# Summing the complex product before the inverse transform, in every second inverse step of an SSM-convolution and gated-MLP block

## The chip, the cores and the metric

The kernel runs on one core of a Trainium2 chip. The metric is device time in microseconds, the median of several executions. The engines that matter here are TensorE (PE in the profile; its weight loads are PEld), VectorE (DVE), ScalarE (ACT), GpSimd (POOL) and the DMA queues that SyncE (SP) issues.

## What is computed

The reference is a block with two branches, cut here to what matters (2048 positions, 640 channels, everything in bfloat16 from outside):

```python
def _A_ref(q, k, v, shift_k, ssm_k, ssm_D):          # long convolution, gated by q
    k_shift = sum over t of k shifted by t * shift_k[:, ks - 1 - t]     # 4 taps   (cut)
    kv = k_shift * v
    kv_f = rfft(kv padded to 2 S)                     # along the sequence, float32
    kf_f = rfft(ssm_k padded to 2 S)
    y = irfft(kv_f * kf_f)[:S]                        # the complex product
    y = y + kv * ssm_D
    return q * y

h = _layernorm(x) * (1 + ca) + sa                     # ca, sa, ga, ... from silu(c) @ w_mod
x = x + ga * _A_ref(h, A_k, A_v, A_shift_k, A_ssm_k, A_ssm_D)
h = _layernorm(x) * (1 + cb) + sb
x = x + gb * _B_ref(h, ...)                           # gelu MLP with a [S, S] spatial mix
```

The change lies in the first branch: in the complex product and the inverse transform that follows it.

## The kernel before

The long convolution is a transform in two stages, written as matmuls. The 640 channels are worked in five units of 128 (`DU`); each unit has eight steps (`NST`) of two frequency blocks (`KP`). For each step, `forward` multiplies the first stage's result by the table `M2` into PSUM, once for the filter (`k_item`) and once for the signal (`u_item`). The filter's result is copied to SBUF as `KH`, in bfloat16. Then VectorE multiplies the signal's real and imaginary parts by the filter's in all four combinations, and TensorE multiplies the four products by the inverse tables `G2` and adds them up in PSUM:

```python
def forward(name, X1, st, extra=()):
    def fn(e):
        pu = new(name, "pu", [P, KP, 2, DU], F32)
        ...
        for k in range(KP):
            kc = st * KP + k
            mm(pu[:, k], M2[:, 0, kc, :], x[:, 2 * kc:2 * kc + 2, :], True, False)
            mm(pu[:, k, 0], M2[:, 2, kc, :], x[:, 2 * kc + 1, :], False, False)
            mm(pu[:, k, 1], M2[:, 1, kc, :], x[:, 2 * kc, :], False, True)
...
def u_item(u, st):
    ...
    def product(e):                                                  # VectorE, line 447
        T_ = new(T, "T", [P, KP, 2, 2, DU])                          # bfloat16
        e.tensor_tensor(T_[:], tl[pu][:, :, :, None, :].to_broadcast([P, KP, 2, 2, DU]),
                        tl[KH][:, :, None, :, :].to_broadcast([P, KP, 2, 2, DU]), op=ALU.mult)
    op("D", "prod", product, r=[pu, KH], w=[T], new=[(T, "T")])

    def inv(e):                                                      # 12 matmuls in a step
        ...
        for k in range(KP):
            kc = st * KP + k
            mm(p_[:, k], G2[:, 0, kc, :], T_[:, k, 0], True, False)          # 256 columns
            mm(p_[:, k], G2[:, 1, kc, :], T_[:, k, 1], False, False)         # 256
            mm(p_[:, k, 1], G2[:, 2, kc, :], T_[:, k, 0, 0], False, False)   # 128
            mm(p_[:, k, 0], G2[:, 1, kc, :], T_[:, k, 0, 1], False, False)   # 128
            mm(p_[:, k, 1], G2[:, 0, kc, :], T_[:, k, 1, 0], False, False)   # 128
            mm(p_[:, k, 0], G2[:, 3, kc, :], T_[:, k, 1, 1], False, True)    # 128
    ...
    op("AD", "zc", ...)      # ScalarE or VectorE copies the result from PSUM into Z
```

Alongside run the four taps and the product with v (`tv`, line 517), a layer norm of x, its modulation `ghm` (line 623: `gh * gca`, then `+ gsa`, on GpSimd or VectorE), a multiplication of `gh` by the inverse transform's result (`ym`, line 640), and a residual add `res` (line 660, GpSimd or VectorE). For the last unit the result Z is transposed on TensorE and kept in tiles `ZT`. Then come the gated MLP's first product (line 237 with `big` and `Z`), its spatial mix (line 918) and its output product (line 936).

All matmuls of the first part go through one helper (`mm`, line 237) and all copies through another (`copy`, line 240), so a line of the profile holds several kinds of work and the tile's name tells them apart.

Nothing is scheduled while it runs: every piece of work is recorded as an operation with the engines that may run it ("GD" is GpSimd or VectorE), and a long list `ORDER` says, operation by operation, on which engine it goes and in which order the engines get their work:

```python
FILLS = (4, 4, 4, 1, 2, 1, 1, 1, 3, 1, 2, 2, )       # matmuls without a use, placed by ORDER
SLOTS = dict(X=4, X1=4, KH=9, T=4, Z=3, ZT=1, wm=1, big=2, dg=2, st1=2, s1=1, sm=2, pu=2, pz=2)
ORDER = """
D13 D95 D12 D96 S14 D97 ...                          # (cut: 991 entries)
"""
```

`SLOTS` gives the number of buffers of each kind.

Of the kernel before, what the change touches and what calls it, by code (L numbers as in the profile page):

```python
# [10 lines left out]
ALU = mybir.AluOpType  # L11
# [4 lines left out]
P = 128  # L16
# [9 lines left out]
DU = 128  # L26
# [7 lines left out]
FILLS = (4, 4, 4, 1, 2, 1, 1, 1, 3, 1, 2, 2, )  # L34
SLOTS = dict(X=4, X1=4, KH=9, T=4, Z=3, ZT=1, wm=1, big=2, dg=2, st1=2, s1=1, sm=2, pu=2, pz=2)
# [4 lines left out]
D13 D95 D12 D96 S14 D97 D103 D109 D104 D110 A0 D115 A5 A4 A1 A2 A3 A111 D98 A99 D6 D18 P979 P980 P981 P19 S16 A112 P21  # L40
D7 D8 D9 S77 D81 S78 A10 D11 G124 G125 D20 P139 A106 D82 D141 P142 A105 A140 A144 P982 P145 A146 D22 G31 D143 D116
D121 A100 G101 A118 S15 P983 P25 S17 D26 P148 S467 P23 D24 S27 A117 G107 A150 P127 D128 A149 A147 S29 G102 P984 P151
A152 P153 A154 S28 G113 S30 G119 P133 A120 G108 P157 A158 P985 P163 S79 A164 P165 A166 D471 D472 P130 D134 P155 A156
G114 P159 A131 D473 D474 P36 G43 D135 P161 D37 A160 P38 D39 P986 P167 D168 A162 A169 G129 P170 A172 P34 A171 S80 P176
A177 D178 P173 D175 P32 A174 S83 P179 D35 P187 P136 D85 P211 D180 D33 G132 P181 S468 D188 D182 A212 P191 P215 P189
A216 D192 S41 A190 P203 D204 P217 A218 P193 A194 D137 P195 S40 D196 P207 S42 P213 D208 D138 P46 P183 D184 P50 A475
P199 S84 A476 D477 D47 A214 P205 A206 P197 D200 A198 P235 A236 P221 D478 A222 D51 P44 P239 A240 P219 A220 D479 G480
P209 A210 P237 S470 D486 P223 P231 A238 A232 D45 P48 A224 D487 P241 A242 D49 S509 P510 A511 P512 A513 D488 D481 A493
S86 D88 D497 P243 D244 A498 G67 D494 P229 A230 P275 G55 A276 P201 D202 P225 A226 P185 S469 S52 D482 P263 P279 A280
P245 A186 A246 D264 D495 S514 P251 D252 P267 S87 P277 A278 D499 D268 P265 A266 P255 A122 D256 P281 A282 D500 P515 P247  # L50
D248 A483 D496 P517 D516 D537 P289 A290 D518 P299 A300 A489 P253 D254 S53 S54 P269 G616 D484 D485 G556 D490 G491 P301
A302 P62 P233 A234 D123 P227 D63 D492 A270 A228 P60 P303 P283 A304 P295 A284 D501 D502 D61 A296 P249 G558 P305 A505
S519 P293 D506 P287 A288 D507 A294 P56 A250 D57 S65 D503 P58 D59 D504 P297 A306 S89 P291 D91 P520 D535 A298 G539 P307
A292 D308 D521 G540 P339 A340 A508 G541 G536 P271 P522 D523 P257 D272 G599 P319 D320 P341 A342 P309 A310 D258 P315
D316 P343 A344 P335 D336 P68 P345 S66 D69 P273 A274 G538 D542 P259 G557 D260 P321 S64 P285 A346 D322 D562 S543 P544
D545 G563 P72 D73 A286 G595 P261 A262 P546 P347 A348 D547 P331 D332 D620 S90 P363 A364 P548 D560 P337 A338 P317 A318
G559 D549 P367 P550 D551 G554 A368 P359 A360 P327 D328 D552 G597 P70 P369 P361 A362 G655 G656 P311 P329 A330 P323 D370
D312 D324 P74 D75 D71 P351 A352 D651 S697 P365 A366 P325 A326 P357 A358 S92 D94 P333 A334 S564 D561 P565 D566 G618
G598 P371 D372 S76 S93 P403 A404 P349 A350 P567 D568 G657 D596 P313 P355 P569 A356 G619 P387 D570 G593 A314 P407 G553
A408 D388 P379 D380 P571 D572 P373 A374 P405 A406 P375 D376 P381 G578 D581 P409 A410 P391 A382 P353 D392 A354 D579  # L60
P389 G573 D576 P427 A428 P395 S601 G653 D654 A390 P377 A378 D396 P429 D600 P399 D400 P397 P383 D384 G594 S698 P602
D603 G583 A430 P431 S524 A432 P423 A424 D587 P401 A402 P415 A416 P433 A434 G588 G617 P604 D577 D575 D398 D605 P425
A426 P411 A412 D652 P393 D574 A394 P435 D436 P419 A420 P606 D607 P385 G658 P451 D452 P443 D444 D582 P608 P437 D438
A386 P417 A418 P525 P421 A422 P447 G614 G615 A526 S622 P453 A454 D609 D613 D448 P455 D456 P445 A446 P463 D464 P449
P459 P457 D460 D580 G611 G621 A450 P413 D610 A414 P623 D624 P439 D440 A458 P465 P625 D626 P461 D462 A466 P441 S527
A442 P627 D628 P528 A529 P665 D666 S530 P663 D664 P629 D630 P659 P661 D662 D631 D632 D633 A660 P987 P667 D668 P676
G555 D669 P683 D670 D671 D699 P690 D700 D672 D684 P531 A532 P533 D634 G701 D702 D703 D704 P705 D673 A534 D706 D674
D715 P988 P713 A714 P711 D712 P989 P709 A710 G636 D675 D635 P707 D708 P990 P763 A764 P731 A732 D716 D677 D640 D637
P759 G717 D718 D691 D720 D719 D678 P729 A730 P723 A724 D681 A760 P741 A742 P765 D682 D784 D679 P725 A726 D639 D641
P727 A728 P761 D781 D680 A766 G646 P721 A722 D638 D783 D782 D586 D648 G785 D786 D787 A788 D789 A762 P738 D790 A739  # L70
S791 P734 P767 A768 D685 D686 P773 A774 A735 P745 A746 D688 P752 A753 P755 A756 D687 D736 A792 D743 P748 G612 A794
D642 A749 D740 D744 P769 D584 D643 D847 P771 A772 D793 D795 D796 P825 A826 A770 D585 P839 A840 P797 A798 D644 P837
A838 P807 P814 A808 D692 P827 A828 A815 P833 A834 D689 P829 A830 D696 D849 D757 D592 D645 P835 A836 D848 D850 G851
D695 D852 D853 D855 D856 D854 D809 S857 P804 A805 D694 D733 D590 D914 D589 D647 P800 A801 D754 P831 A832 D693 D913
D650 A858 D816 D859 D860 D861 P811 A812 P821 A822 P818 D862 P866 P887 D649 A819 P863 A888 A864 D916 D591 D915 G917
P870 D806 A871 D918 D919 D920 D922 D921 A867 P877 D813 D817 D868 P899 D758 D872 A900 P905 A878 A906 D747 S923 D925
D924 D750 P880 A881 A927 D928 P873 A874 D875 P901 D802 A902 P903 A904 D810 D926 P884 A885 P929 A930 P946 D820 D823
A947 P932 A933 D876 P893 A894 D882 P939 P950 D751 A940 P959 P957 D737 G775 A951 A958 D879 D883 A960 D799 P897 A898
D934 P943 A944 D803 D824 D776 D889 D777 D886 G841 D842 P953 A845 P936 A937 A954 A780 P963 A964 D948 D846 P895 A896
A843 D778 P969 D890 P971 A972 D865 D869 G907 D908 D911 D909 D910 A970 P891 A892 A779 P967 P965 A966 D912 D955 D952  # L80
D956 D938 D945 D949 D941 D942 D931 D935 G973 A844 D974 A977 D976 D975 A126 P961 A962 A968 D978
# [39 lines left out]
def kernel(  # L121
# [80 lines left out]
    with ExitStack() as actx:  # L202
# [56 lines left out]
        mbase = consta.tile([P, KCH, QH], F32, name="mbase")  # L259
# [10 lines left out]
        nc.gpsimd.iota(mbase[:], [[4, KCH], [64, QH]], base=1, channel_multiplier=0, allow_small_or_imprecise_dtypes=True)  # L270
# [44 lines left out]
        def m2_base():  # L315
            def steps(e):
                e.tensor_scalar(mstep[:, 0:NCH], fidx[:, 0:NCH], pidx[:, 0:1], 4.0 * KCH / 8192.0, op0=ALU.mult, op1=ALU.mult)
                e.tensor_scalar(mstep[:, NCH:], mstep[:, 0:NCH], 0.25, None, op0=ALU.add)
                e.tensor_scalar(mturn[:], mstep[:], TWO_PI, None, op0=ALU.mult)
            op("D", "mstep", steps, w=["mstep"])  # L320
            op("D", "mbase", lambda e: e.tensor_scalar(mbase[:], mbase[:], pidx[:, 0:1], 1.0 / 8192.0, op0=ALU.mult, op1=ALU.mult),
               w=["mbase"])

        def m2_chunk(i):
# [4 lines left out]
            def turns(e):  # L329
                new(a, "T", [P, 2, KCH, QH], F32)  # L330
                for h in range(2):
                    e.tensor_scalar(tl[a][:, h], mbase[:], mstep[:, h * NCH + i:h * NCH + i + 1], MAGIC, op0=ALU.add, op1=ALU.add)
            op("DG", "turns", turns, r=["mbase", "mstep"], w=[a], new=[(a, "T")])
            op("D", "msub", lambda e: e.scalar_tensor_tensor(tl[a][:], tl[a][:], MAGIC, mbase[:, None].to_broadcast([P, 2, KCH, QH]),
# [104 lines left out]
        def u_item(u, st):  # L439
# [4 lines left out]

            def product(e):
                T_ = new(T, "T", [P, KP, 2, 2, DU])
                e.tensor_tensor(T_[:], tl[pu][:, :, :, None, :].to_broadcast([P, KP, 2, 2, DU]),  # L447
                                tl[KH][:, :, None, :, :].to_broadcast([P, KP, 2, 2, DU]), op=ALU.mult)
            op("D", "prod", product, r=[pu, KH], w=[T], new=[(T, "T")])

            def inv(e):
# [4 lines left out]
                for k in range(KP):  # L456
                    kc = st * KP + k
                    mm(p_[:, k], G2[:, 0, kc, :], T_[:, k, 0], True, False)
# [6 lines left out]
               r=[T] + [("G2", i * 2 + st * KP // 8) for i in range(4)] + ([(Z, "new")] if st else []),  # L465
               w=[pz] + ([] if st else [(Z, "new")]), new=[(pz, "pz")] + ([] if st else [(Z, "Z")]))
# [203 lines left out]
        def last_stage_pe(u):  # L670
# [3 lines left out]
            for b, qb in enumerate(range(0, NQ, QB)):  # L674
                pt, ZT = "pt%d_%d" % (u, qb), "ZT%d_%d" % (u, qb)
                ZTs.append(ZT)
# [6 lines left out]
                def keep(e, pt=pt, ZT=ZT):  # L683
                    new(ZT, "T", [P, QB, P])
# [301 lines left out]
```

## Time and profile before

| | |
|---|---|
| time, median of 3 | 337.06 us (336.98 to 337.31) |
| span of the profiled execution | 335.4 us |
| TensorE busy | 320.8 us (96%) |
| VectorE busy | 222.7 us (66%) |
| ScalarE busy | 140.2 us (42%) |
| GpSimd busy | 72.7 us (22%) |
| mean granted TensorE clock | 0.995 |
| product, line 447 | 40 instructions, 1217 ns each |
| inverse step, 12 matmuls | 0.88 us on the chain |
| forward step, 6 matmuls | 0.44 us on the chain |
| first and last inverse step begin | 31.5 us and 133 us |

How to read it: the convolution with everything beside it takes about the first 142 us, the MLP's first product the time to 207 us, and the spatial mix with the output product the rest. Busy shares are averages over all three. A group in the profile gives its line, engine and operation, then output and inputs by the program's names with partitions and elements, how often it runs, its busy time and the mean of one, and after the bar the idle time of its engine just before it and what ended that. The chain is followed back from the last instruction, at each step to what released it. Matmuls overlap one another, so their single durations are longer than their spacing; the chain shows the spacing.

### The profile page before, as it was taken

Reading aid. Unit: us, or ns where it says so; the run is one execution under the profiler, and the core shown is the slowest. Engines: PE = TensorE matmul, PEld = TensorE weight load, DVE = VectorE, ACT = ScalarE, POOL = GpSimd, SP = SyncE. Lnnn points to the kernel's source line nnn. Section 1 sums busy time; section 2 is a strip of 40 time slices with the busy share of each in tenths; the row PEclk is TensorE's granted clock in tenths of the full one; section 3 lists DMA queues with packets and bytes.
Section 4 is the critical chain, followed back from the end, with each engine's and each line's share of the span. In section 5 each row is a group of like instructions: output and inputs, shape, how many; then the busy total and the mean of one; then the engine's idle time right before and its main releaser. Section 6 shows DMA issues by size and latency. Waiting matters only on the chain.

```text
span 335.4 us, 6584 instructions
## 1 busy us (share of the span) xinstructions
PE 320.8 (96%) x2712; PEld 214.3 (64%) x2719; DVE 222.7 (66%) x468; ACT 140.2 (42%) x242; POOL 72.7 (22%) x89
## 2 busy tenths in 40 slices
PE   6799999999989999999999999999999999999995
PEld 1467879878879899845555555555555555555553
DVE  7987999899999999997885775263222332223323
ACT  2774999975657754257765669000000000000000
POOL 2560040447694903222101121000000000000000
PEclk9999999999999999989999999999999999999999
DMA  8999998999767836302145900995555657532221
GB/s 143 183 201 228 217 309 202 251 215 242 173 143 157 264 64 163 102 2 48 32 78 79 191 0 3 215 220 132 118 117 121 133 131 131 110 49 47 49 47 59
DMA packets 128581, 45.00 MB, mean 134 GB/s; under 512 B 117704, under 2 KB 127784, under 8 KB 128552
## 3 DMA queue, kind: packets, MB, share of 16 engines
q1 hardware_dynamic: 126592, 44.59, 61.5%
q8 instruction: 21, 0.34, 0.4%
q10 hardware_dynamic: 1960, 0.01, 0.3%
q14 instruction: 8, 0.07, 0.1%
HBM read 16.11 MB, written 5.24 MB: 64 GB/s over the span
## 4 chain that ended last, share of the span: by engine, by line
PE 73%; DVE 17%; DMA 5%; issue 2%; POOL 1%; ACT 0%; DVEq 0%; SPq 0%; ACTq 0%
PE ps L918 28%; PE pz L237 15%; PE pu L237 14%; PE po L936 9%; DVE T L447 5%; PE sm L237 4%; PE s L237 2%; DVE big L517 2%; DMA D_col<-in_A_ssm_D_dram 2%; DMA big<-in_A_k_dram 1%; DMA X<-kv_scr 1%; DVE X L240 1%; DVE gh L623 1%; DVE st L666 1%; DMA kv_scr<-big 1%
## 5 line engine op out<-in xcount | busy, mean ns | idle before, releaser
L918 PE MATMUL ps<-X,wT 128*128 128x432 bf16 x512 | 95.7, 346 | 0.0
L918 PEld LDWEIGHTS <-wT 128*128 128x128 bf16 x512 | 50.0, 98 | 42.2
L929 ACT COPY uT<-pt 128x896 bf16<-128x896 bf16 x1 | 0.9, 905 | 116.9 <-PE pt L928 116.9
L237 PEld LDWEIGHTS <-Z 128*128 128x128 bf16 x320 | 31.1, 98 | 27.7 <-issue 1.1
L447 DVE TENSOR_TENSOR T<-pu,KH 128x1024 bf16<-128x1024 f32 x40 | 47.7, 1217 | 1.4 <-PE pu L237 1.0
L237 PE MATMUL pu<-X,M 128*128 128x128 bf16 (+1 forms) x480 | 45.5, 237 | 0.8 <-DVE T L447 0.7
L237 PE MATMUL pz<-T,G 128*128 128x128 bf16 (+1 forms) x480 | 41.2, 237 | 0.7 <-DVE T L447 0.6
L237 PEld LDWEIGHTS <-M 128*128 128x128 bf16 x480 | 37.1, 98 | 6.2 <-issue 1.3
L921 DVE SCALAR_TENSOR_TENSOR u<-ps,bcol,G 128x432 bf16<-128x432 f32 x18 | 12.0, 668 | 42.2 <-PE ps L918 42.2
L237 PEld LDWEIGHTS <-G 128*128 128x128 bf16 x480 | 35.3, 98 | 3.6 <-DVE T L447 0.8
L240 ACT CAST X<-s 128x1024 bf16<-128x1024 f32 x31 | 31.5, 1015 | 11.2 <-PE s L237 11.0
L936 PE MATMUL po<-w_o,uT 128*128 128x320 bf16 (+1 forms) x224 | 32.8, 299 | 0.0
L237 PE MATMUL pz<-big,Z 128*128 128x432 bf16 x160 | 32.3, 346 | 0.5 <-ACT M L856 0.5
L237 PE MATMUL pu<-big,Z 128*128 128x432 bf16 x160 | 32.6, 347 | 0.0
L921 DVE SCALAR_TENSOR_TENSOR u<-ps,bcol,M 128x432 bf16<-128x432 f32 x14 | 9.3, 667 | 29.5 <-PE ps L918 29.5
L936 PEld LDWEIGHTS <-uT 128*128 128x128 bf16 (+1 forms) x224 | 21.8, 98 | 9.8
L240 ACT CAST KH<-pu 128x512 bf16<-128x512 f32 x40 | 22.9, 596 | 10.1 <-PE pu L237 10.0
L938 DVE TENSOR_TENSOR ot<-po,xt 128x320 bf16<-128x320 f32 x32 | 15.7, 491 | 13.4 <-PE po L936 13.4
L240 ACT CAST Z<-pz 128x512 bf16<-128x512 f32 x32 | 18.6, 590 | 10.4 <-PE pz L237 10.0
L862 DVE BATCH_NORM_STATS2 stz<-X 128x6 f32<-128x432 bf16 x32 | 18.2, 586 | 6.8 <-ACT X L856 6.8
L237 PE MATMUL sm<-big,dg 128*128 128x512 bf16 (+3 forms) x73 | 20.0, 380 | 1.3 <-DVE big L517 0.5
L623 POOL TENSOR_TENSOR gh<-gh,gca_bf 128x512 bf16<-128x512 bf16 x14 | 16.8, 1202 | 16.9 <-DVE gca_bf L610 12.9
(141 smaller groups left out, 380.6 us busy)
## 6 DMA issues: line engine op xcount, KB each, us to landing
wm<-in_w_mod_dram SPq DMA_DIRECT2D x6, 800.0 KB, 5.8
xt<-in_A_q_dram SPq DMA_DIRECT2D x4, 640.0 KB, 6.3
out_dram<-ot SPq DMA_DIRECT2D x16, 160.0 KB, 2.3
big<-in_B_w_in_dram SPq DMA_DIRECT2D x2, 1080.0 KB, 6.9
X<-in_A_ssm_k_dram SPq DMA_DIRECT2D x4, 512.0 KB, 8.7
kv_scr<-big SPq DMA_DIRECT2D x4, 512.0 KB, 3.4
X<-kv_scr SPq DMA_DIRECT2D x4, 512.0 KB, 5.2
w_o<-in_B_w_out_dram SPq DMA_DIRECT2D x6, 160.0 KB, 3.0
```

Of the source, the lines that this page charges most:

```text
L237: nc.tensor.matmul(o, lhsT=w, rhs=x, start=start, stop=stop)
L240: (e.copy if e is nc.scalar else e.tensor_copy)(dst, src)
L447: e.tensor_tensor(T_[:], tl[pu][:, :, :, None, :].to_broadcast([P, KP, 2, 2, DU]), tl[KH][:, :, None, :, :].to_broadcast([P, KP, 2, 2, DU] ...
L517: e.tensor_tensor(vsl, tl[ps][:], vsl, op=ALU.mult)
L623: lambda e, vec=vec, o=o: e.tensor_tensor(gvu, gvu, vec[:, None, d0:d0 + du].to_broadcast([P, TB, du]), op=o),
L666: op("D", "ln2", lambda e, n=n: e.bn_stats(out=st2[:, n, (0, 0, 0, 1, 2)[u], :], in_=xt[:, n, us[0] * DU:(u + 1) * DU]), r=[("xt", (v, n)) ...
L862: op("D", "stz", lambda e, i=i, n=n, fc=fc: e.bn_stats(out=stz[:, n, fc, :], in_=tl[z2][:, i, fc * FC:(fc + 1) * FC]), r=[(z2, (i, fc))], ...
L918: nc.tensor.matmul(ps[:, :FC], lhsT=wTs[t][:, s_, :], rhs=tl["z2_%d" % (s_ // TB)][:, s_ % TB, fc * FC:(fc + 1) * FC], start=(s_ == 0), st ...
L921: nc.vector.scalar_tensor_tensor(u[:, sl], ps[:, :FC], bcol[:, t:t + 1], z1[t][:, sl], op0=ALU.add, op1=ALU.mult)
L929: nc.scalar.copy(uTs[t][:], pt[:])
L936: nc.tensor.matmul(ps[:, :HS], lhsT=uTs[t][:fsz[ft], ft, :], rhs=w_o[:fsz[ft], ft, h * HS:(h + 1) * HS], start=(ft == 0), stop=(ft == NFT ...
L938: nc.vector.tensor_tensor(ot[:, h * HS:(h + 1) * HS], ps[:, :HS], xt[:, t, h * HS:(h + 1) * HS], op=ALU.add)
```

## The change

In a step whose number is in `SUMS` (1, 3, 5, 7: every second one), the four products are kept in float32, and two additions form the real and the imaginary part of the complex product before it is rounded to bfloat16. TensorE then multiplies two parts, not four, by the inverse tables: 6 matmuls in the step and not 12. The aim is to take work from TensorE and give it to GpSimd and VectorE. The other steps stay as they were.

```diff
-FILLS = (4, 4, 4, 1, 2, 1, 1, 1, 3, 1, 2, 2, )
-SLOTS = dict(X=4, X1=4, KH=9, T=4, Z=3, ZT=1, wm=1, big=2, dg=2, st1=2, s1=1, sm=2, pu=2, pz=2)
+FILLS = (4, 4, 4, 2, 1, 1, 1, 3, 1, 1, 3, 1, 2, )
+SUMS = (1, 3, 5, 7)
+SLOTS = dict(Tf=2, W=2, X=3, X1=4, KH=9, T=3, Z=3, ZT=1, wm=1, big=2, dg=2, st1=2, s1=1, sm=2, pu=2, pz=2)
...
+            summed = st in SUMS
+            ttag = "Tf" if summed else "T"
             def product(e):
-                T_ = new(T, "T", [P, KP, 2, 2, DU])
+                T_ = new(T, ttag, [P, KP, 2, 2, DU], F32 if summed else BF16)
...
+            if summed:
+                def total(e, o):
+                    if o == 0:
+                        new(W, "W", [P, KP, 2, DU])
+                    T_ = tl[T]
+                    e.tensor_tensor(tl[W][:, :, o, :], T_[:, :, 0, o, :], T_[:, :, 1, 1 - o, :],
+                                    op=ALU.add if o else ALU.subtract)
+                op("GD", "csum", lambda e: total(e, 0), r=[T], w=[(W, 0), (W, "new")], new=[(W, "W")])
+                op("GD", "csum", lambda e: total(e, 1), r=[T, (W, "new")], w=[(W, 1)])
...
                 for k in range(KP):
                     kc = st * KP + k
+                    if summed:
+                        w_ = tl[W]
+                        mm(p_[:, k], G2[:, 0, kc, :], w_[:, k], True, False)
+                        mm(p_[:, k, 1], G2[:, 2, kc, :], w_[:, k, 0], False, False)
+                        mm(p_[:, k, 0], G2[:, 1, kc, :], w_[:, k, 1], False, True)
+                        continue
```

To make room for the float32 products (`Tf`), buffers are moved: `X` has 3 and not 4, `T` 3 and not 4, the last unit's `ZT` tiles go into `X` buffers and not into `T`, and a table used at the start (`mbase`) goes into a `KH` buffer. The list `ORDER` is a new one throughout, so a number of other operations change their place or their engine too. In it 30 of the 40 additions stand on GpSimd and 10 on VectorE. Of the operations that were there before, five casts of Z and five second norms go from VectorE to ScalarE, and two residual adds from GpSimd to VectorE; some ten others move by one or two.

## The prediction

> **What bounds the kernel now.** I read the busy shares first, then the chain that ended last, then busy time by stage, then who waited for whom in the stage that changes. Page, busy time by engine, and the chain's shares:
>
> ```profile
> PE 320.8 (96%) x2712; PEld 214.3 (64%) x2719; DVE 222.7 (66%) x468; ACT 140.2 (42%) x242; POOL 72.7 (22%) x89
> ...
> PE 73%; DVE 17%; DMA 5%; issue 2%; POOL 1%; ACT 0%; DVEq 0%; SPq 0%; ACTq 0%
> ```
>
> On these two lines alone TensorE is the bound, and anything taken from it would come off the time. But both are averages over the whole span. The same by stage (columns after the stretch: its length, then busy time and instructions of PE, weight loads, VectorE, ScalarE, GpSimd):
>
> ```profile
> 0.00:28.00 28.00, 21.81 (x146) 12.20 (x148) 22.70 (x64) 15.79 (x33) 11.45 (x26) 1.00 0.95 177
> 28.00:57.00 29.00, 28.82 (x319) 24.25 (x319) 28.22 (x52) 23.80 (x39) 3.88 (x4) 1.00 1.04 249
> 57.00:90.00 33.00, 32.21 (x367) 26.90 (x369) 30.48 (x56) 25.49 (x42) 16.73 (x16) 1.00 0.99 220
> 90.00:114.00 24.00, 22.21 (x286) 19.45 (x286) 23.71 (x27) 14.75 (x22) 19.54 (x17) 1.00 0.78 179
> 114.00:142.00 28.00, 27.66 (x510) 25.51 (x508) 26.59 (x46) 12.56 (x22) 8.78 (x10) 0.99 0.49 128
> 142.00:157.00 15.00, 13.70 (x80) 7.18 (x78) 13.71 (x41) 9.95 (x19) 5.06 (x7) 0.91 0.01 2
> 157.00:207.00 50.00, 50.00 (x276) 26.80 (x274) 36.87 (x112) 34.51 (x64) 7.21 (x12) 1.00 0.42 72
> 207.00:335.40 128.40, 124.42 (x743) 72.00 (x740) 40.37 (x77) 3.34 (x6) 0.00 (x0) 1.00 0.51 110
> ```
>
> From 157 us to the end TensorE runs alone (50.00 of 50.00, then 124.42 of 128.40) and the change doesn't touch it. All that changes lies in the first 142 us, and there two engines are full at once: from 28 to 142 us PE is busy 28.82 + 32.21 + 22.21 + 27.66 = 110.9 of 114 us, VectorE 28.22 + 30.48 + 23.71 + 26.59 = 109.0. A busy PE is modelled time; what counts is how long VectorE stands still because of it. The waits of VectorE from 28 us to the last inverse step at 134 us (engine and line, what it waited for, us in total, times, longest):
>
> ```profile
> DVE nmr L564 <- POOL rstd L183: 1.3, 1, 1.3
> DVE X L240 <- PE pu L237: 1.3, 1, 1.3
> DVE T L447 <- PE pu L237: 1.0, 4, 0.4
> DVE gh L640 <- PE sm L237: 0.4, 1, 0.4
> ```
>
> So in 106 us VectorE waited for TensorE 1.3 + 1.0 + 0.4 = 2.7 us. That is about the most that a faster TensorE can give in this stage as long as VectorE's own work stays what it is.
>
> The rows that price the change (busy, mean ns of one | idle before):
>
> ```profile
> L447 DVE TENSOR_TENSOR T<-pu,KH 128x1024 bf16<-128x1024 f32 x40 | 47.7, 1217 | 1.4 <-PE pu L237 1.0 <-issue 0.2
> L237 PE MATMUL pz<-T,G 128*128 128x128 bf16 x320 | 30.9, 220 | 0.0
> L237 PE MATMUL pz<-T,G 128*128 128x256 bf16 x160 | 30.6, 273 | 0.7 <-DVE T L447 0.6
> L334 DVE SCALAR_TENSOR_TENSOR T<-T,mbase 128x512 f32<-128x512 f32 x4 | 2.7, 686 | 0.0
> L623 POOL TENSOR_TENSOR gh<-gh,gsa_bf 128x512 bf16<-128x512 bf16 x14 | 16.5, 1182 | 3.5 <-DVE gh L623 2.4 <-DVE gsa_bf L613 1.0
> L623 DVE TENSOR_TENSOR gh<-gh,gsa_bf 128x512 bf16<-128x512 bf16 x6 | 5.1, 843 | 0.0
> ```
>
> The means of 220 and 273 ns are latencies and overlap. The chain in order of time has the real spacing: an inverse step of 12 matmuls is 0.88 us on it, a forward step of 6 matmuls 0.44 us. The last row matters too: the same operation takes 410 ns at best on VectorE, 843 in the mean and 1358 at worst.
>
> **What the Trainium skill says.** (1) "SBUF — State Buffer", section "Who interferes with whom": a VectorE instruction with two SBUF inputs shares a read port with GpSimd, and whichever comes second stands until the first is done. The trace agrees: the 843 ns above against 410, and values near 1358, which is 410 plus most of one GpSimd instruction of 1182. (2) "GPSIMD Engine Reference", section "3.1 Elementwise — side-by-side cycle accounting": about 2.6 cycles per element for a two-input operation at 1.2 GHz[...], which is 1.11 us for 512 elements; the trace has 1.18. (3) "VectorE: DVE Perf Modes", section "The perf-mode tier table": a two-input operation runs at one element per cycle if an operand is in PSUM or is float32. So the product costs the same with a float32 output; the trace has 1217 ns for 1024 elements with a PSUM operand, 686 for 512 in float32 from SBUF, on one straight line.
>
> **The change, part by part.**
>
> *TensorE.* In 20 of the 40 inverse steps (4 of 8 in each of 5 units) 12 matmuls with 2048 columns become 6 with 1024, the size of a forward step: 0.88 to 0.44 us, 20 x 0.44 = 8.8 us. Two more filler matmuls (28, not 26) of 512 columns at about 0.22 us (four times 512 columns of the taps stand as 0.86 on the chain) give back 0.4. Net -8.4 us of TensorE work.
>
> *The sums.* 40 new instructions of 256 elements; in the changed program's order 30 stand on GpSimd and 10 on VectorE. On GpSimd one is half of 1182 and a little for its start, say 0.62 us (estimate): 30 x 0.62 = 18.6 us on an engine that was busy 48.9 of the 114 us. On VectorE the line through 1217 (1024 elements) and 686 (512) has 1.04 ns per element and 0.15 us fixed, so 0.42 us: 10 x 0.42 = 4.2.
>
> *Moves.* The new order shifts work from VectorE to ScalarE. VectorE: casts of Z 8 to 3 (5 x 0.68 = -3.4), second norms 15 to 10 (5 x 0.44 = -2.2), one copy less in the last unit's transposes (-0.7), two more residual adds (2 x 0.41 = +0.8), and some ten moves by one instruction that sum to about -0.7. With the sums: 4.2 - 3.4 - 2.2 - 0.7 + 0.8 - 0.7 = -2.0 us. ScalarE takes on some 12 us; it was busy 76.6 of the 114 us, so it has room.
>
> *The shared port.* What VectorE loses to GpSimd now: 6 x (608 - 415) and 6 x (843 - 415) ns of the two modulation steps, 8 x (529 - 410) of the residual adds, about 1.0 us of one add of D (1178 against 218 ns): 1.2 + 2.6 + 1.0 + 1.0 = 5.7 us over 26 exposed instructions, 0.22 each. Afterwards 38 are exposed (10 sums and 2 adds more), and GpSimd works there some 62 us in place of 49: 38 x 0.22 x 62/49 = 10.6. The new GpSimd instructions are half as long, so they hold VectorE up for less; I take 9. That is +3.3 us on VectorE.
>
> *Latency and buffers.* Between product and inverse step there now lie two sums, 1.24 us if both are on GpSimd. In the new order the TensorE work between the forward and the inverse step of a summed item is 3 us or more in 19 of 20 cases (2.2 in the last), against 1.22 + 1.24 = 2.5 needed, so this is covered unless GpSimd is behind. X has 3 buffers in place of 4; each is still free 20 us or more of TensorE work before its next reader, against 5.2 us (from the scratch) and 8.7 us (from the input) for the load. I expect nothing from it.
>
> *Sum.* VectorE sets this stage. Gain: 2.7 us of waiting for TensorE, and 2.0 of work less. Loss: 3.3 us at the port. Net -1.4 us; with 337.06 before, **335.7 us**. Of 8.4 us taken off TensorE I expect a sixth to reach the time.
>
> **The rivals.** *TensorE is the bound after all*: the chain's 73% speaks for it, and in the new order all waits can be placed anew. Then the whole 8.4 us comes off: 328.7. Against it stand 109.0 busy us of VectorE in 114. A part of it could come from the first 28 us, where VectorE was idle for 5.3; the new order, counted with the same rows, puts some 5 us more VectorE work ahead of the first inverse step. That would add 2 to 3 us of gain: 332 to 333. *GpSimd becomes a link*: the sums stand in its queue behind modulation steps and residual adds of 1.2 us, and each sum that comes late stops TensorE and then everything. Half a microsecond in each of 20 steps is 10 us: 345. Against it: the distance of 3 us and more. *The port costs more than I took*: if every VectorE sum waits for a whole GpSimd sum and the modulation steps always hit, VectorE gets 7 us more in place of 3.3, and the time is about 339.
>
> **Range and chances.** My sum has two terms of 2 to 5 us with opposite signs, each unsure by half. The port's rival ends at 339, and the better-filled start at 332. I take 331 to 340. Faster by over 2% is below 330.3 and needs TensorE to be the bound almost wholly: 0.12. Slower by over 2% is above 343.8 and needs GpSimd to hold up TensorE: 0.07. The rest, 0.81, is within 2%.
>
> **What would show it.** Right: PE busy lower by some 8 us in the first 142 us but idle more, waiting for VectorE; VectorE busy 97% or more from 28 us to the last inverse step; the float32 product still near 1217 ns; GpSimd's sums near 0.62 us; VectorE's sums well above 0.42 in the mean; everything from 157 us on unchanged in length. Wrong: if VectorE also shows gaps of several us that end with GpSimd's sums, the second rival holds; if the last inverse step ends 6 us or more earlier, VectorE wasn't the bound.

## The result, and the profile after

The changed kernel takes 341.37 us (340.28 to 341.53, 4 runs) against 337.14 us (336.98 to 337.31, 4 runs): 1.0118 of the time before, 95% interval 1.0097 to 1.014. It is slower by 4.2 us, though by my estimate TensorE has 8.4 us less to do. I had predicted 335.7 us.

The page after, busy time by engine, and the chain's shares (the chain stops at 147 us, so its shares don't add up to the span):

```profile
PE 316.3 (93%) x2592; PEld 207.6 (61%) x2601; DVE 227.8 (67%) x467; ACT 149.5 (44%) x260; POOL 89.8 (26%) x113
...
PE 53%; DMA 1%; ACT 1%; DVE 1%; issue 0%; ACTq 0%
```

TensorE gave up 4.5 us of modelled busy time in the whole span; VectorE got 5.1 us more, GpSimd 17.1. By stage (length, then PE, weight loads, VectorE, ScalarE, GpSimd, and the granted TensorE clock):

```profile
28.00:57.00 29.00, 26.84 (x283) 22.02 (x283) 27.02 (x52) 26.30 (x48) 12.29 (x17) 1.00 0.88 218
57.00:90.00 33.00, 30.52 (x341) 24.99 (x342) 32.79 (x55) 24.59 (x38) 19.04 (x20) 1.00 0.95 197
90.00:114.00 24.00, 19.61 (x261) 17.01 (x261) 23.91 (x28) 16.31 (x24) 18.56 (x16) 1.00 0.74 161
114.00:142.00 28.00, 25.24 (x391) 22.55 (x389) 25.81 (x36) 14.99 (x26) 16.34 (x18) 0.94 0.61 175
...
211.00:339.10 128.10, 124.10 (x741) 71.81 (x739) 40.86 (x78) 2.57 (x4) 0.00 (x0) 1.00 0.43 93
```

Between 57 and 114 us VectorE is busy 32.79 + 23.91 = 56.7 of 57 us, TensorE only 30.52 + 19.61 = 50.1 (before: 54.2 and 54.4). TensorE has time to spare, VectorE none. The last stage has its old length. What TensorE waits for there (waits of PE from 28 us to the last inverse step at 136.8 us):

```profile
PE pu L240 <- DVE T L456: 3.7, 4, 1.8
PE pu L240 <- DVE Tf L456: 2.7, 3, 1.7
PE s L240 <- DVE X L395: 2.0, 2, 1.4
PE pz L240 <- DVE W L465: 1.2, 2, 1.0
```

All four lines name VectorE: forward steps that wait for a PSUM buffer which the product still has to read, a first-stage step, and inverse steps that wait for a sum. Behind the longer wait of the third, though, lies a load: that VectorE instruction itself waited 1.4 us for X from DMA. GpSimd's sums are not among them. The rows of the new and the slower instructions (busy, mean ns | idle before):

```profile
L456 DVE TENSOR_TENSOR Tf<-pu,KH 128x1024 f32<-128x1024 f32 x20 | 24.0, 1214 | 0.8 <-issue 0.4 <-PE pu L240 0.3
L465 POOL TENSOR_TENSOR W<-Tf 128x256 bf16<-128x256 f32 x30 | 21.5, 737 | 36.6 <-DVE Tf L456 36.6
L465 DVE TENSOR_TENSOR W<-Tf 128x256 bf16<-128x256 f32 x10 | 9.3, 951 | 0.1
L648 DVE TENSOR_TENSOR gh<-gh,gsa_bf 128x512 bf16<-128x512 bf16 x5 | 5.6, 1129 | 0.0
```

The float32 product costs what the bfloat16 one did (1214 ns). A sum on VectorE takes 951 ns in the mean; the same instruction takes 409 at best (409 / 1055 / 1375 least, median, most). So ten sums cost 9.3 us, more than half of it waiting inside the instruction. The second of the two modulation steps on VectorE went from 843 to 1129 ns.

The ten sums are far from alike, and the trace shows what the long ones meet (start, us, engine):

```profile
57.51 0.41 DVE L465 TENSOR_TENSOR W<-Tf 128x256 bf16<-128x256 f32 x1
...
108.23 1.33 POOL L685 TENSOR_TENSOR xt<-xt,gh 128x512 bf16<-128x512 bf16 x1
108.48 2.67 DVE L465 TENSOR_TENSOR W<-Tf 128x256 bf16<-128x256 f32 x2
109.53 1.34 POOL L648 TENSOR_TENSOR gh<-gh,gca_bf 128x512 bf16<-128x512 bf16 x1
111.07 1.37 DVE L648 TENSOR_TENSOR gh<-gh,gca_bf 128x512 bf16<-128x512 bf16 x1
113.63 0.60 PE L240 MATMUL pu<-X,M 128*128 128x256 bf16 x6 [1.73 <-DVE Tf L456]
```

Three sums, at 57.5, 63.8 and 70.5 us, run while GpSimd stands still and take 0.41 or 0.42 us. One at 86.1 us, beside three of GpSimd's own sums, takes 0.67. The other six come in twos, at 93.1, 108.5 and 133.9 us, beside an unbroken row of GpSimd's residual adds and modulation steps, and take 2.67, 2.67 and 2.03 us for two. At 108 us the delay goes on to TensorE: it waits 1.73 us for the next product and soon after 0.53 us for another. From 114 to 120 us its granted clock was then 0.72 in the mean, where the kernel before had 1.00, and in this stretch VectorE stood still for 0.7 us, waiting for TensorE, and for 0.4 us more. Whether TensorE's standstill brought the lower clock on was not tested.

Where the 3.7 us of span lie (335.4 to 339.1): the last inverse step ends at 136.8 us and not at 133.9 (+2.9); the first MLP matmul begins 13.2 us after that and not 12.0 (+1.2); the rest gives 0.4 back.

### The profile page after: what moved, and what is told of

It reads as the page before. It is cut to its first block, busy times and chain, and to the rows that moved or that the text cites. A ratio compares the mean times of both kernels' runs of the same rounds, so it can differ in the third digit from the quotient of the medians.

```text
span 339.1 us, 6399 instructions
## 1 busy us (share of the span) xinstructions
PE 316.3 (93%) x2592; PEld 207.6 (61%) x2601; DVE 227.8 (67%) x467; ACT 149.5 (44%) x260; POOL 89.8 (26%) x113
## 4 chain that ended last, share of the span: by engine, by line
PE 53%; DMA 1%; ACT 1%; DVE 1%; issue 0%; ACTq 0%
PE ps L945 28%; PE po L963 9%; PE pu L240 8%; PE pz L240 8%; DMA Z<-Z 1%; ACT Z L858 0%; PE sm L824 0%; PE s L240 0%; DVE u L948 0%; DVE gh L727 0%; ACT Z L831 0%; DVE ot L965 0%; PE pt L955 0%; DVE xt L685 0%; ACTq L831 0%
## 5 line engine op out<-in xcount | busy, mean ns | idle before, releaser
L240 PE MATMUL pu<-X,M 128*128 128x128 bf16 (+1 forms) x480 | 47.2, 240 | 6.7 <-DVE T L456 3.7
L240 PEld LDWEIGHTS <-M 128*128 128x128 bf16 x480 | 38.4, 99 | 13.7 <-issue 8.6
L240 PE MATMUL pu<-big,Z 128*128 128x432 bf16 x160 | 33.4, 354 | 0.0
L465 POOL TENSOR_TENSOR W<-Tf 128x256 bf16<-128x256 f32 x30 | 21.5, 737 | 36.6 <-DVE Tf L456 36.6
L240 PEld LDWEIGHTS <-G 128*128 128x128 bf16 x360 | 27.0, 98 | 3.7 <-DVE W L465 1.3
L243 ACT CAST KH<-pu 128x512 bf16<-128x512 f32 x40 | 23.0, 594 | 13.8 <-PE pu L240 13.2
L243 ACT CAST Z<-pz 128x512 bf16<-128x512 f32 x37 | 21.4, 592 | 10.2 <-PE pz L240 10.2
L965 DVE TENSOR_TENSOR ot<-po,xt 128x320 bf16<-128x320 f32 x32 | 15.7, 492 | 13.4 <-PE po L963 13.4
L456 DVE TENSOR_TENSOR Tf<-pu,KH 128x1024 f32<-128x1024 f32 x20 | 24.0, 1214 | 0.8 <-issue 0.4
L456 DVE TENSOR_TENSOR T<-pu,KH 128x1024 bf16<-128x1024 f32 x20 | 24.2, 1214 | 0.0
L240 PEld LDWEIGHTS <-X 128*128 128x128 bf16 x288 | 18.0, 98 | 7.6 <-DVE X L395 3.4
L240 PE MATMUL s<-F1bd,X 128*128 128x256 bf16 x128 | 19.7, 278 | 2.1 <-DVE X L395 2.0
```

The costliest lines, as they stand in the source:

```text
L240: nc.tensor.matmul(o, lhsT=w, rhs=x, start=start, stop=stop)
L243: (e.copy if e is nc.scalar else e.tensor_copy)(dst, src)
L465: e.tensor_tensor(tl[W][:, :, o, :], T_[:, :, 0, o, :], T_[:, :, 1, 1 - o, :], op=ALU.add if o else ALU.subtract)
L965: nc.vector.tensor_tensor(ot[:, h * HS:(h + 1) * HS], ps[:, :HS], xt[:, t, h * HS:(h + 1) * HS], op=ALU.add)
```

## The experiments

My theory: VectorE sets the stage, and its ten sums are the loss, partly by their own work and partly by the port that it shares with GpSimd. Rivals: late sums on GpSimd hold TensorE up; or the new order and buffers are worse whatever the sums do.

### 1. The ten sums of VectorE moved to GpSimd

```diff
-... D259 ... D268 ... D289 ... D350 ... D330 D331 ... D403 ... D422 ... D474 D475
+... G259 ... G268 ... G289 ... G350 ... G330 G331 ... G403 ... G422 ... G474 G475
```

> The changed kernel, but all 40 additions stand on GpSimd (the ten that stood on VectorE changed engine, not place). In the changed kernel those ten cost VectorE 9.3 us. If the port between VectorE and GpSimd on a full VectorE is the cause (theory), VectorE loses 9.3 us, gets back 1 to 3 us from more collisions, and the time falls from 341.4 to 335 to 338. If late sums on GpSimd are what holds TensorE up (rival), the time rises to 343 or more. If the new order and buffers are the cause whatever the sums do (second rival), it stays at 341.

Measured: 333.42 us, 0.9894 of before (0.9858 to 0.993); a second time beside later runs 332.85 us, 0.9876 (0.986 to 0.9892), where 333 to 334 was expected:

> The first experiment's kernel again, beside the others on the same chip: 333 to 334.

Nothing but the engine of ten instructions of 256 elements is changed, and it is worth some 8 us. The time fell further than to the 335 to 338 that I expected; the 9.3 us of the sums, less 1 to 3 for collisions, would have made 333 to 335. The kernel is now faster than both, in the changed kernel's own order and buffers, so these are not the cause of the loss. The stage from 57 to 114 us in this run:

```profile
57.00:114.00 57.00, 55.30 (x681) 47.51 (x684) 55.00 (x83) 45.53 (x70) 44.40 (x46) 1.00 0.93 199
```

TensorE is back at 55.30 us: it does in these 57 us the work of 681 matmuls, 600 in the changed kernel. GpSimd works 44.40 us, and TensorE waits for its sums for 0.7 us in all. The rival of late sums on GpSimd falls.

### 2 to 4. Sums left out; inverse steps of the two lengths in the two orders

Run 2 leaves the sums out of the changed kernel and lets the six matmuls read two of the four products. Run 3 leaves them out and has twelve matmuls everywhere, in the new order. Run 4 is the kernel before with six matmuls left out in every second step. Runs 2 and 4 don't compute the convolution. Runs 2 and 3 have five buffers for the bfloat16 products (`Tf=5`), in the space of the two float32 ones and `W`, since without the sums a buffer is held until its inverse step.

```diff
 # runs 2 and 3
-SLOTS = dict(Tf=2, W=2, ...
+SLOTS = dict(Tf=5, W=2, ...
-                T_ = new(T, ttag, [P, KP, 2, 2, DU], F32 if summed else BF16)
+                T_ = new(T, ttag, [P, KP, 2, 2, DU], BF16)
-                    e.tensor_tensor(tl[W][:, :, o, :], ...)
+                    return
 # run 2                                 # run 3
-                        w_ = tl[W]     -                    if summed:
+                        w_ = T_[:, :, 0]   +                    if False:
 # run 4, in the kernel before
+                    if st % 2:
+                        mm(p_[:, k], G2[:, 0, kc, :], T_[:, k, 0], True, False)
+                        mm(p_[:, k, 1], G2[:, 2, kc, :], T_[:, k, 1, 0], False, False)
+                        mm(p_[:, k, 0], G2[:, 1, kc, :], T_[:, k, 1, 1], False, True)
+                        continue
```

> The changed kernel's order with the additions left out: the product is bfloat16 and the six matmuls of a summed step read two of the four products (the result is then not the convolution). TensorE keeps its relief, VectorE and GpSimd lose the sums (9.3 and 22 us) and the collisions. Theory: 331 to 334. Second rival (the order itself): 339 or more.

> The changed kernel's order with the additions left out and all steps with twelve matmuls again, so the arithmetic of the kernel before in the new order. Theory: VectorE is relieved by some 12 us against the changed kernel, TensorE has its 8.8 us again, so about the kernel before: 335 to 338. Second rival (the order itself is worse): 341 or more.

> The kernel before, in its own order, with six of the twelve matmuls left out in every second inverse step and nothing else changed (the result is then not the convolution). It takes 8.8 us of work off TensorE and gives nothing to anybody. If VectorE sets this stage (theory), only its 2.7 us of waiting for TensorE can come off: 334.5 to 336. If TensorE is the bound (rival), 328 to 330.

| us (ratio to before, interval) | twelve matmuls everywhere | six in every second step |
|---|---|---|
| old order, no sums | 336.93 (the kernel before) | 335.16 (0.9952, 0.9937 to 0.9967) |
| new order, no sums | 337.78 (1.0029, 1.0016 to 1.0042) | 331.58 (0.984, 0.9824 to 0.9856) |

All three came as the theory had it. Three things follow. The new order without sums is worse than the old by 0.3% only, about 1 us, so it doesn't explain the loss. In the old order the same 8.8 us of TensorE work are worth under 2 us: the chain's 73% of TensorE was no promise. In the new order, with the five buffers of runs 2 and 3, they are worth 6.2 us. The stage shows why. From 57 to 114 us in run 3, then the same in run 4:

```profile
57.00:114.00 57.00, 56.34 (x696) 48.97 (x699) 53.92 (x79) 44.32 (x67) 34.96 (x31) 1.00 0.90 195
```

```profile
57.00:114.00 57.00, 51.42 (x606) 43.03 (x608) 54.61 (x84) 40.09 (x63) 37.30 (x33) 1.00 0.97 209
```

In run 3 TensorE is full (56.34) and VectorE has slack, so relief reaches the time. In run 4 TensorE runs idle (51.42) and VectorE still works 54.61. The likely reason for the difference is that the new order had moved casts and norms from VectorE to ScalarE; no run moves these alone. The ten sums on VectorE took the gain away again. VectorE's waits for TensorE point the same way beforehand: from 28 to 150 us they are 3.3 us in the kernel before (1.3 + 1.0 + 0.6 + 0.4) and 7.0 us in run 3, most of it in these lines:

```profile
DVE gh L661 <- PE sm L240: 3.5, 5, 1.3
...
DVE Tf L456 <- PE pu L240: 2.0, 3, 1.1
DVE T L456 <- PE pu L240: 0.7, 1, 0.7
```

These waits don't vanish with the relief. In run 4 some 2.3 us of them are left and in run 2 3.3, so they fell by 1.0 and 3.7 us while the time fell by 1.8 and 6.2. They were a ceiling in both cases, not the sum of what went.

Run 2 against experiment 1 also prices all 40 sums on GpSimd: 333.42 or 332.85 against 331.58, some 1 to 2 us. Put together, the runs lead from the kernel before to the changed one: about +1 us for the new order, -6.2 for TensorE's relief, +1 to +2 for forty sums on GpSimd, and +8 for having ten of them on VectorE.

### 5 and 6. The work of ten sums, and the port, apart

Both are experiment 1 with ten extra VectorE instructions of 256 float32 elements, where the changed kernel has its ten sums; what they compute is thrown away. They differ in the operation: statistics have one SBUF input and write six elements, the addition has two inputs and writes 256.

```diff
+                    if (u, st, o) in EXTRA:       # the ten places
+                        nc.vector.bn_stats(out=<scrap>, in_=T_[...])                                  # run 5
+                        nc.vector.tensor_tensor(<scrap>, T_[:, :, 0, o, :], T_[:, :, 1, 1 - o, :], op=ALU.add)    # run 6
```

> All 40 sums on GpSimd as in the first experiment, and on VectorE, in the places where the changed kernel has its ten sums, ten extra instructions of the same size with one SBUF input (statistics over 256 float32 elements, thrown away). They cost VectorE time but don't use the port it shares with GpSimd: near 0.41 us each in any company. If VectorE is full, 10 x 0.41 = 4.1 us on top of the first experiment's 333.4: 336.5 to 338. If VectorE's own work doesn't matter, 333 to 334.

> As the run with one input, but the ten extra instructions are additions of two float32 SBUF inputs (256 elements, thrown away), the form of the sums themselves. Theory (port): 0.42 us of work each, but 0.9 us or more in the trace because of GpSimd, so 4 to 6 us above the run with one input: 340.5 to 343. If the ten sums cost what their work is and no more, it is level with it.

Measured: 336.36 us with one input (0.9989, 0.9974 to 1.0003), 341.23 us with two (1.0139, 1.01 to 1.0177). The first lies just below the 336.5 to 338 that I expected. The groups of the extra instructions and their least, median and longest times in ns, run 5 and run 6:

```profile
L469 DVE BATCH_NORM_STATS2 stz<-Tf 128x6 f32<-128x256 f32 x10 | 4.2, 421 | 0.2
L469 DVE BATCH_NORM_STATS2 stz<-Tf x10: 414/422/428, 59.4 to 131.6; 128x6 f32<-128x256 f32 x10
```

```profile
L469 DVE TENSOR_TENSOR gb_bf<-Tf 128x256 bf16<-128x256 f32 x10 | 7.7, 770 | 0.2
L469 DVE TENSOR_TENSOR gb_bf<-Tf x10: 411/824/1261, 57.9 to 135.0; 128x256 bf16<-128x256 f32 x10
```

Against 332.85 in the same batch the ten instructions' own work costs 3.5 us (4.2 in the trace): on this full VectorE work goes nearly one to one into the time. Alone the two forms take the same, 414 and 411 ns; beside GpSimd only the addition is stretched. That costs 4.9 us more and brings the kernel to where the changed one is. The trace shows 3.5 of those 4.9 in the extra instructions themselves. The rest goes with a lower granted clock in run 6: of its four executions three have a mean of 0.98 or 0.99, and executions of the two runs with the same mean clock lie only 3.0 to 3.8 us apart. As in the changed kernel, the clock was 0.72 from 114 to 120 us in run 6, and it was 1.00 there in run 5, whose profiled execution had 0.94 from 28 to 57 us instead. If these ten instructions stand for the ten sums, a good 3.5 us of the 8 are work and about as much is the wait inside the instruction, with a last part of 1 us or so that goes with the lower clock. That it is the read side of the port, and not the writing of 256 elements, these two runs don't separate.

### 7. Two residual adds taken out of the way of the norm

In experiment 1 the last inverse step ends well before the kernel before's, but the first MLP matmul lags. On that path, in order of time (start, us, engine), experiment 1:

```profile
136.98 2.26 POOL L685 TENSOR_TENSOR xt<-xt,gh 128x512 bf16<-128x512 bf16 x2
137.04 1.11 DVE L800 SCALAR_TENSOR_TENSOR nmr<-mv,rstd 128x2 f32<-128x2 f32 x1 [0.24 <-POOL rstd L186]
138.07 1.35 DVE L812 TENSOR_SCALAR Z<-xt,mv,rstd 128x640 bf16<-128x640 bf16 x1
```

VectorE works on two elements for 1.11 us, then on a norm for 1.35, until GpSimd's two adds are over.

```diff
-... G652 G677 ...      # the two residual adds
+... D652 D677 ...
```

> All 40 sums on GpSimd, and the two residual adds that GpSimd has between the inverse stage and the first MLP matmul done on VectorE in their place in the order, which is behind the first norms. In the trace of the first experiment these two adds (2.26 us together) stand just as VectorE's small scale instruction (1.11 us, 0.16 when alone) and its norm (1.35 us, 0.44 when alone) want to run, on the path to the first MLP matmul. Theory: 1.9 us less until then, 0.8 us more VectorE work later that is hidden: 331.3 to 332.5. If the norm's wait is hidden by something else, no change.

Measured: 332.18 us (0.9862, 0.9835 to 0.9888) beside 332.85; a second time 331.64 us (0.9826, 0.9807 to 0.9846):

> The version with all sums on GpSimd and two adds moved, again, beside the other on the same chip: 331.5 to 332.5.

The same two instructions in this run:

```profile
137.92 0.16 DVE L800 SCALAR_TENSOR_TENSOR nmr<-mv,rstd 128x2 f32<-128x2 f32 x1 [0.23 <-POOL rstd L186]
137.99 0.44 DVE L812 TENSOR_SCALAR Z<-xt,mv,rstd 128x640 bf16<-128x640 bf16 x1
```

0.95 and 0.91 us are gone, as expected. The first MLP matmul comes 11.2 us after the last inverse step's copy begins (141.2 less 130.0) and not 13.4 (142.6 less 129.2). Most of it is lost again: the last MLP matmuls of the stage begin at 202.2 us against 202.7. In the batch where both ran, the intervals overlap; a gain of this edit by itself isn't shown. Of the versions that compute the block it has the lowest times, well below both kernels.

### 8. Five modulation steps moved to GpSimd as well

```diff
-... D579 D581 ... D635 ... D598 ... D641 ...
+... G579 G581 ... G635 ... G598 ... G641 ...
```

> The version with all sums on GpSimd and two adds moved, and now also the five additions of the modulation that VectorE still had go to GpSimd, in their place in the order. VectorE loses 5 instructions that took 0.86 us each in the first experiment (4.3 us), GpSimd gets 5 x 1.17 = 5.9 us, in a stretch where it is already busy 22.0 of 24 us (90 to 114 us). If only VectorE's time counts: 2 to 4 us less than the version before, 328 to 330. If GpSimd is now the limit (its sums come late and stop TensorE): 333 or more.

Measured: 334.4 us (0.9926, 0.9908 to 0.9945) beside 331.64 for version 7: worse. Waits of TensorE for GpSimd's sums from 28 to 145 us, this run and then version 7 in the same batch:

```profile
PE pz L240 <- POOL W L465: 2.8, 3, 1.4
```

```profile
PE pz L240 <- POOL W L465: 0.8, 1, 0.8
```

From 90 to 114 us GpSimd is now busy 23.6 of 24 us and its sums come late more often. VectorE's loss of work no longer helps. This fits the second rival of the prediction, one step further on than the change went. It is not shown in full: the two executions in these traces took the same time, 333.52 and 333.56 us (the second was the slowest of its seven), so the 2.0 us of added waits are a sign and don't measure the 2.8 us between the medians.

## Why the prediction was wrong

**The bound: right for the old order.** VectorE sets this stage. I said that a faster TensorE could give at most its 2.7 us of waiting in the order of the kernel before; run 4 gave 1.8. But I carried these 2.7 us over to the new order, where run 3 has 7.0 us of such waiting and up to 6.2 us came off. So the first rival, TensorE as the bound, was mostly true for the new order without its sums (6.2 of 8.8 us). (One reading was loose: from 157 us on TensorE is full, but not alone; VectorE works 36.87 of 50 us there.)

**TensorE's saving: right.** Summed steps take half the time. The first 142 us have some 7 us less PE busy time, but they also hold less of the work now; up to the first MLP matmul it is 5.3 us less (136.6 to 131.3).

**The product in float32: right** (1214 ns). **GpSimd's sum: too low**, 737 ns and not 620. It did little harm by itself: GpSimd had the room.

**The shared port: the step that failed.** I put it at +3.3 us. I spread the loss of the kernel before evenly, 0.22 us for each exposed instruction, and then took something off because GpSimd's sums are short. From 28 to 137 us the trace of the changed kernel has, mean less shortest: 10 x (951 - 409) for the sums, 5 x (1129 - 410) and 7 x (547 - 407) for the modulation steps, 3 x (974 - 411) for the adds, and for the first norms 11 x (554 - 436), against their mean before: 5.4 + 3.6 + 1.0 + 1.7 + 1.3 = 13.0 us, against 5.7 before. That is +7.3 and not +3.3. Evenly was wrong. GpSimd's short sums do hold VectorE up for little, as I had it (0.67 us beside them), but six of the ten sums stand beside GpSimd's long adds and modulation steps where these follow one another without a pause: a sum takes 0.41 us away from them and 1.0 to 1.3 us beside them, in the mean of two. In six pairs one half stood on each engine, but that is not what makes the collisions: the VectorE halves took 0.41, 0.42, 0.41, 0.67 and 2.67 us for the last two, and the four sums of the two pairs wholly on VectorE took 1.2 us in the mean.

Up to the first MLP matmul (145.9 us before, 150.0 after) VectorE is busy 5.0 us longer (135.2 to 140.2), where my -2.0 of work and +3.3 at the port make +1.3. The work came out near what I had, or a little lower; the port is the difference.

**The waiting that I counted as gain: not gained.** Between 28 us and the last inverse step VectorE stood still for 4.2 us in the kernel before (105.9 less 101.7) and for 4.3 us in the changed one (108.8 less 104.5); its busy share there is 96% in both, where I expected 97% or more. Its waits for TensorE became shorter (2.7 to 1.7 us), but a wait of 1.4 us for a load of X came in, from which I had expected nothing. Up to the first MLP matmul it stood still for 0.9 us less, and I had counted 2.7.

**What I left out: the way to the MLP.** I had nothing in the sum for it; the new order placed a norm against two adds of GpSimd (1.35 us in place of 0.44) and lost 1.2 us there, of which the norm's own delay is 0.9. Experiment 7 shows the collision and what it hides.

**The rivals.** The one that says the port costs more than I took was the true one: it had 7 us at the port, and 7.3 came. I had put its time at 339, because it still counted the 2.7 us of waiting as gained; of these only 0.9 came. Of the better-filled start little came: VectorE is busy 23.2 of the first 28 us, and was 22.7.

## What to carry to other kernels

When two engines are full, price a change on both: the time that the other waits for it was the better guide to what work taken off one can give (VectorE's 3.3 and 7.0 us of waiting against gains of 1.8 and 6.2, two cases), not its share of the chain, and that time has to be read in the order that will run. Before you put an operation with two SBUF inputs on VectorE, look at what GpSimd does at that moment: price it at its lone time where GpSimd pauses (0.41 us here) and at a multiple beside an unbroken row of its operations (1.0 to 1.3). GpSimd can take such operations as long as it has room. A very long small instruction, two elements in 1.11 us, was the mark of a collision here: look at what the neighbour runs at that time.

## What the runs showed that I had not expected

The sum on GpSimd has a fixed part that I took too small: the medians of 729 ns for 256 elements and 1157 for 512 in the same trace make 1.7 ns for each element and about 0.3 us to start. That is an estimate from two points which differ in type as well, float32 inputs in the sums and bfloat16 in the modulation. And VectorE's one-tensor norm in bfloat16 is held up by GpSimd too (438 to 1354 ns), not only instructions with two tensors: the first norms took 554 ns in the mean, where they had 436.
